# Attention into an MLP on one core: q and k of four first blocks loaded in 1 KB packets, turned 64 columns at a time, and the mask counts spread by TensorE

## The chip, the cores and the metric

One Trainium2 chip, one of its cores. The metric is device time in microseconds for one execution of the whole program. The kernel before took 602.19 us, the median of three runs (601.85, 602.19, 604.92). Its profiled execution took 602.55 us; the profiled span inside it is 600.8 us. Engines are named as in the profile: PE (TensorE; PEld its weight loads), DVE (VectorE), ACT (ScalarE), POOL (GpSimd), SP (SyncE, which here only issues DMAs).

## The reference

```python
batch, n_heads, seq, head_dim = (4, 8, 768, 64); n_global, n_local = (8, 96)
def _attn_ref(q, k, v, n_global, n_local):
    scores = np.matmul(q, k.transpose(0, 1, 3, 2)) / np.sqrt(D)
    rel = pos[:, None] - pos[None, :]
    is_global = pos[None, :] < n_global
    is_local = (rel >= 0) & (rel < n_local)
    keep = is_global | is_local
    dist = np.where(is_global & ~is_local, n_local, np.abs(rel))
    scores = scores - slopes[:, None, None] * dist     # slopes = 2 ** -(h + 1), 8 heads
    a = softmax(np.where(keep, scores, -1e9))
    return np.matmul(a, v)
def _moe_ref(x, w_in, w_out):                          # x (3072, 512), w_in (512, 2048), w_out (2048, 512)
    h = x @ w_in
    return (h / (1 + np.exp(-1.702 * h))) @ w_out
```

q, k and v are fp32 of shape (4, 8, 768, 64), so one row of a head is 64 numbers, 256 B, and four rows that follow each other are 1 KB. The weights lie in memory as 64-bit words. `n_local` and `n_global` are 64-bit integers in memory, and the masks are made from them on the chip.

## The kernel before, in words

The sequence of each batch is cut into six blocks of 128 positions, 24 blocks in all. Every query needs the keys of its own block, of the block before, and the first `n_global` keys. The four first blocks of the batches (n = 0 to 3, `n < EARLY` and `n < FIRST`) need their own block alone, and are done first, in fp32 (`prep_first`, `first`). The other twenty are done later with fp16 pairs and DMA transposes (`prep`, `unit`). After two blocks are finished, their 256 rows are a chunk of the MLP: `up` (tile h) and `down` (tile y) run over eight slices of the weights, and from the third chunk on `up_two` and `down_two` take their place.

Each step is a `Task` with the engines that may do it and an estimated price; it is added to a list by `add`. `Work.order` then plays the list through with the estimates and due times (shifted by the table `NUDGE`), and writes the instructions of every engine in the order that comes out. Each engine keeps this order on the chip and waits where data or a buffer isn't ready. Where PE finds nothing ready in the first 50 us of that plan, `order` puts in a spare pair of products on constant data (tile `idle`, line 1056), whose result nobody reads.

For a first block `prep_first` does this. `load` issues one DMA on SP for q and one for k, from `(q, k)[b, :, 128 rows, :]` to the tile `raw` with a position in each partition and the eight heads behind each other; each packet is a row of 256 B. `turn` (line 422) turns two heads at a time, four transposes of 128x128 for q and four for k, into the PSUM tile `tq` (two such buffers, ring `r_h`, shared with the spares and with h). `taken` (line 429) scales and copies: q goes to `QZ` in two halves (its upper 64 partitions and its lower 64, each to its own columns; POOL has written zeros between), one by ACT and one by DVE; k goes to `KF` (its buffers are named hl) whole, by ACT. Then `first` makes the scores of four heads at a time (tile s, line 604, fp32, with the mask added by a bf16 product, line 605), their maxima on DVE (`top`), a transpose of those (`aux`), the scores again turned (sT), their exponentials on ACT (pt, line 636), and the products with v (pv).

The masks: POOL writes the positions (`places`), DVE turns them into distances. `ci` holds the two counts, read by two DMAs on ACT's queue into all 128 partitions. `counts` (lines 308 to 311) makes `cnt` of them, `own` the mask of the own block, `other` that of the block before; `slopes` multiplies by each head's slope, with line 338 on ACT and line 340 on DVE: eight 128x128 masks for the first blocks (M1, four on each engine) and eight 128x256 masks for later blocks (M2, on DVE).

The weights come by SP, 1 MB at a time (ws), and are made into fp16 pairs by steps on DVE and ACT (lines 370 to 378, tiles wa and w).

Of the kernel before, what the change touches and what calls it, by code (L numbers as in the profile page):

```python
# [8 lines left out]
F32 = mybir.dt.float32  # L9
# [3 lines left out]
I32 = mybir.dt.int32  # L13
# [6 lines left out]
P = 128  # L20
# [6 lines left out]

NUDGE = {"T2": -1.5, "down02": 1.4, "down05": -8.2, "down07": -0.8, "down103": 6.7, "down113": -5.5,  # L30
# [4 lines left out]

NG = 8
SKIP = 24
EARLY = 4

FIRST = 4  # L40
SIGN = [{"DVE": 0.62, "ACT": 1.0}]
TURN_X = 4
WARM, GAP = 50.0, 0.5
AHEAD = 24.0
BACKLOG = 3.0
# [42 lines left out]
class Work:  # L88
# [15 lines left out]
    def order(self):  # L104
# [17 lines left out]
                        t.due, moved = due, True  # L122
        for t in self.tasks:
            t.due += NUDGE.get(t.tag, 0.0)
        free = dict.fromkeys(("PE", "DVE", "ACT", "POOL", "SP"), 0.0)
        dma, now, done = 1.5, 0.0, []
        worked, spared = 0.6, 0
# [2 lines left out]
        while len(done) < len(self.tasks) + spared:  # L130
            moved = False
            for e in free:
                if free[e] > now or (e == "SP" and dma > now + BACKLOG):
                    continue
                best = None
                for t, at in ready.items():
                    if e not in t.on or at > now or t.early() > now or (best is not None and t.due >= best.due):
                        continue
                    us = t.on[e]
                    if any(max(free[o], now) + c < now + us for o, c in t.on.items() if o != e):  # L140
                        continue
# [12 lines left out]
                if best is None:  # L154
                    if e != "PE" or now > WARM or now < worked + (GAP if worked > 7.0 else 0.0):
                        continue
                    best = self.spare(spared)
                    b = best.bufs[0]
                    if len(b.ring.taken) >= b.ring.bufs and (b.ring.taken[-b.ring.bufs].left or b.ring.taken[-b.ring.bufs].end > now):
                        continue  # L160
                    b.users, b.left = [best], 1
                    ready[best] = now
                    spared += 1
                t, us = best, best.on[e]
# [45 lines left out]
def kernel(  # L210
# [34 lines left out]
    cf = const.tile([P, 2, 2], F32, name="cf")  # L245
# [60 lines left out]

    def counts(e):
        nc.vector.tensor_copy(cf, ci)
# [25 lines left out]
    def slopes(e, js, hs=range(H)):  # L334
        for h in hs:
# [3 lines left out]
            else:  # L339
                nc.vector.tensor_scalar(mm[:, h, js], mk()[:, js], f, None, ALU.mult)  # L340

    wk.tag = "masks"
    m0 = add({"POOL": 2.0}, places, bufs=[ints], want=-9.0)
    m0 = add({"DVE": 1.3}, distances, [m0], [ints, flt, mk], -4.0)
    late = add({"POOL": 1.0}, lambda e: None, [m0], want=0.0)
    m0 = add({"DVE": 0.65}, counts, [m0, late])
    covers = add({"DVE": 1.2}, covered, [m0])
    covers.soon = 300.0
    m1 = add({"DVE": 1.1}, own, [m0], [flt, mk])
# [45 lines left out]
    def load(n, raw, parts=(0, 1, 2)):  # L395
        b, i = place(n)
        return [add({"SP": 1.55}, lambda e, z=z: nc.sync.dma_start(
            raw()[:, z], (q, k, v)[z][b, :, i * P:(i + 1) * P, :].rearrange("h p d -> p h d")), bufs=[raw]) for z in parts]

    def guard(n, raw, ld, want):  # L400

        for z, us in ((0, 1.06), (1, 0.63)):
# [5 lines left out]
    def prep_first(n):  # L408
# [3 lines left out]
        KF = Buf(r_hl, [P, NU, P], F32, f"KF{n}", lambda t: t.bitcast(F32).rearrange("p (u t) -> p u t", u=NU))  # L412
        d = blk[n] = dict(QZ=QZ, KF=KF, sm=Buf(r_sm, [P, 2 * H], F32, f"sm{n}"))
        zero = add({"POOL": 1.0}, lambda e: [nc.gpsimd.memset(QZ()[D * z:D * z + D, :, 1 - z, :], 0.0) for z in range(2)], bufs=[QZ])
        ld = load(n, raw, (0, 1))
        turned = []
        for z in range(2):
            tq = Buf(r_h, [P, NU, P], F32, f"tq{n}_{z}")

            def turn(e, z=z, tq=tq):  # L420
                for u in range(NU):
                    nc.tensor.transpose(tq()[:, u], raw()[:, z, 2 * u:2 * u + 2, :].rearrange("p h d -> p (h d)"), ident)

            turned.append((tq, add({"PE": 4 * TURN}, turn, ld[z:z + 1], [raw, tq])))

        def taken(to, z, part):
            tq, t1 = turned[z]
            return add({"ACT": 0.6, "DVE": 0.7}, lambda e: (
                nc.scalar.mul(to(), tq()[part], SX) if e == "ACT" else nc.vector.tensor_scalar(to(), tq()[part], SX, None, ALU.mult)),
                [t1], [tq, KF if z else QZ])  # L430

        rows = [slice(D * z, D * z + D) for z in range(2)]
        d["qk_ready"] = [zero, *(taken(lambda z=z: QZ()[rows[z], :, z, :], 0, rows[z]) for z in range(2)), taken(KF, 1, slice(0, P))]

    def own_values(n):

# [82 lines left out]
    def unit(n, u, want_s, want_v):  # L519
# [27 lines left out]
        d.setdefault("S", []).append(t1)  # L547
        ex = []
        for j in range(2):
            t2 = add({"DVE": 0.365}, lambda e, j=j: rows(e, j), [t1, M2], [sp, pr])  # L550
# [30 lines left out]
    def first(n, want):  # L581
# [15 lines left out]
        for f in range(2):  # L597
# [6 lines left out]
                        nc.tensor.matmul(sp()[:, j], qp, kp, start=(z == 0), stop=False, skip_group_check=True)  # L604
                    nc.tensor.matmul(sp()[:, j], id16, mm[:, h, 2], start=False, stop=True, skip_group_check=True)

            t1 = add({"PE": 4 * (mm_s + MM128)}, scores, [M1[f], *d["qk_ready"]], [sp, *QKs], want + 1.2 * f)
            d.setdefault("S", []).append(t1)
            maxed.append(add({"DVE": 0.61}, lambda e, f=f, sp=sp: nc.vector.tensor_reduce(
                top[:, n, 4 * f:4 * f + 4], sp(), axis=AX.X, op=ALU.max, negate=True), [t1], [sp]))  # L610
# [656 lines left out]
```

## Time and profile before

| what | value |
|---|---|
| median of the runs | 602.19 us |
| profiled execution | 602.55 us, span 600.8 us, mean granted clock of TensorE 0.997 |
| busy shares | PE 98%, PEld 74%, DVE 84%, ACT 78%, POOL 1% |
| DMA packets | 268502, of which 249536 under 512 B; 109.58 MB |
| queue q10, on which the counts come | 288 packets |
| loads of q and k in this form | 24 each, 256 KB each (four of each for the first blocks) |

A row of a group has the line, the engine, the operation, output and inputs, and how often, then busy time and the mean of one, then the idle time of the engine just before and what ended it. A row in order of time has the start, the duration, and in brackets the idle time before it with its releaser. Bars of matmuls are modelled at their ends: a bar reaches into the next one, so the price of one in a dense row is read from start to start. PEclk in the tables is the granted clock as a share.

### The profile page before, as it was taken

The numbers are of one execution on the slowest core, as the hardware profiler recorded it, in microseconds if no ns is written. First come the engines' busy times: TensorE is split into PE (matmuls) and PEld (weight loads), VectorE is DVE, ScalarE is ACT, GpSimd is POOL, SyncE is SP. The second block draws the span as 40 slices with busy tenths as digits, with TensorE's granted clock in tenths as the row PEclk, the third lists the DMA queues.
The fourth block names the chain that finished last, engine by engine and source line by source line (L and its number), as shares of the span: only waits on it lengthen the run. The fifth ranks groups of instructions, "written<-read, shape, count | busy, mean of one in ns | idle before, by whom it ended". The sixth has DMA issues, their size and how long they took to land.

```text
span 600.8 us, 17038 instructions
## 1 busy us (share of the span) xinstructions
PE 587.3 (98%) x6816; PEld 445.8 (74%) x6816; DVE 502.9 (84%) x1177; ACT 471.6 (78%) x1098; POOL 5.8 (1%) x18
## 2 busy tenths in 40 slices
PE   8989999999999999999999999999999999999995
PEld 5878767776777867777677777777678778867895
DVE  6998999999999999789699789798979978766532
ACT  3878899978758988888688899788989988844432
POOL 3000000000000000000000000000000000000000
PEclk9999999999999999999999999999999999999998
DMA  8998898999976778969996999999989999910001
GB/s 221 316 249 254 235 251 191 196 187 203 198 139 127 160 117 182 199 141 206 194 222 153 227 204 233 206 229 198 240 181 227 227 205 237 231 29 3 36 2 40
DMA packets 268502, 109.58 MB, mean 182 GB/s; under 512 B 249536, under 2 KB 250048, under 8 KB 268416
## 3 DMA queue, kind: packets, MB, share of 16 engines
q1 hardware_dynamic: 268128, 108.43, 85.7%
q8 instruction: 55, 0.90, 0.6%
q14 instruction: 31, 0.25, 0.1%
q10 hardware_dynamic: 288, 0.00, 0.0%
HBM read 57.67 MB, written 6.29 MB: 106 GB/s over the span
## 4 chain that ended last, share of the span: by engine, by line
PE 82%; DMA 7%; ACT 4%; DVE 4%; issue 1%; SPq 1%; DVEq 0%; ACTq 0%
PE y L895 35%; PE pa L827 13%; PE h L787 10%; PE pb L827 10%; PE s L536 4%; DMA pt<-hl 2%; DMA out_dram<-yo 1%; PE s L604 1%; PE pv L567 1%; PE pv L568 1%; PE pv L569 1%; PE sT L623 1%; DMA raw<-in_k_dram 1%; DMA xT<-x 1%; DMA ws_00again<-in_moe_w_in_dram 1%
## 5 line engine op out<-in xcount | busy, mean ns | idle before, releaser
L895 PE MATMUL y<-w,g 128*128 128x512 f16 (+1 forms) x1248 | 266.9, 363 | 0.0
L895 PEld LDWEIGHTS <-g 128*128 128x128 f16 x1248 | 117.9, 98 | 103.3
L827 PEld LDWEIGHTS <-w 128*128 128x128 f16 x1728 | 101.2, 98 | 4.8
L552 ACT ACTIVATE p<-p,NM 128x232 f32<-128x232 f32 x160 | 76.5, 481 | 7.3 <-DVE NM L542 7.1
L827 PEld LDWEIGHTS <-T 128*128 128x128 f16 x1296 | 77.1, 98 | 6.2 <-issue 0.2
L787 PE MATMUL h<-xT,w 128*128 128x256 f16 x576 | 69.4, 273 | 0.5 <-DMA xT<-x 0.5
L542 DVE CUSTOM_DVE_ANT_0 p<-s,mm 128x232 f32<-128x232 f32 x160 | 57.7, 396 | 8.4 <-PE s L536 7.8
L787 PEld LDWEIGHTS <-w 128*128 128x128 f16 x576 | 55.2, 98 | 9.6 <-issue 0.8
L868 DVE SCALAR_TENSOR_TENSOR g<-t,g 128x512 f16<-128x512 f32 x72 | 49.3, 688 | 12.3 <-ACT g L867 12.0
L557 DVE TENSOR_TENSOR hl<-p,hl 128x464 f16<-128x464 f32 x80 | 50.9, 637 | 8.1 <-ACT hl L556 7.9
L867 ACT ACTIVATE g<-t 128x512 f16<-128x512 f32 x72 | 45.0, 628 | 9.5 <-DVE t L860 8.1
L859 ACT ACTIVATE t<-h 128x512 f32<-128x512 f32 (+1 forms) x72 | 35.9, 516 | 18.0 <-DVE h L835 14.9
L556 ACT CAST hl<-p 128x464 f16<-128x464 f32 x80 | 46.1, 577 | 4.2 <-DMA pt<-hl 2.3
L835 DVE TENSOR_TENSOR h<-pb,h 128x256 f32<-128x256 f32 x72 | 29.5, 420 | 22.6 <-PE pb L827 19.3
L827 PE MATMUL pa<-xS,T 128*128 128x128 f16 x648 | 45.0, 219 | 0.1
L860 DVE SCALAR_TENSOR_TENSOR t<-t,h 128x512 f32<-128x512 f32 (+1 forms) x72 | 38.3, 554 | 4.8 <-ACT t L859 4.2
L536 PEld LDWEIGHTS <-QK 128*128 128x128 f16 x640 | 36.4, 98 | 4.3 <-DMA QK<-QK 0.8
L536 PE MATMUL s<-QK 128*128 128x128 f16 x320 | 38.5, 219 | 0.6 <-DMA QK<-QK 0.6
L827 PE MATMUL pb<-xS,w 128*128 128x128 f16 x540 | 37.5, 219 | 0.0
L827 PE MATMUL pa<-xT,w 128*128 128x128 f16 x540 | 37.0, 219 | 0.0
L567 PE MATMUL pv<-VR,pt 128*128 128x64 f16 x288 | 34.8, 193 | 1.3 <-DMA pt<-hl 1.3
L569 PE MATMUL pv<-VR,pt 128*128 128x64 f16 x288 | 34.9, 193 | 0.0
(181 smaller groups left out, 1080.7 us busy)
## 6 DMA issues: line engine op xcount, KB each, us to landing
ws<-in_moe_w_in_dram SPq DMA_DIRECT2D x8, 1024.0 KB
ws<-in_moe_w_out_dram SPq DMA_DIRECT2D x8, 1024.0 KB
raw<-in_q_dram SPq DMA_DIRECT2D x24, 256.0 KB
raw<-in_k_dram SPq DMA_DIRECT2D x24, 256.0 KB
out_dram<-yo SPq DMA_DIRECT2D x22, 256.0 KB
QK<-QK SPq DMA_DIRECT2D x40, 128.0 KB
raw<-in_v_dram SPq DMA_DIRECT2D x20, 256.0 KB
ws_00again<-in_moe_w_in_dram SPq DMA_DIRECT2D x8, 512.0 KB
```

The lines of the kernel that those rows point to most:

```text
L536: nc.tensor.matmul(sp()[:, j, lo:hi], d["QK"]()[:, 0, h, :], K[:, 1 + z, h, P - (hi - lo):], start=(z == 0), stop=(z == 1), skip_group_che ...
L542: nc.vector.tensor_tensor_reduce(out=pr()[:, j, :], in0=sp()[:, j, :], in1=m, scale=-1.0 / SC, scalar=3.0e38, op0=ALU.add, op1=ALU.min, ac ...
L552: ex.append(add({"ACT": 0.473}, lambda e, j=j: nc.scalar.activation(pr()[:, j, :], pr()[:, j, :], AF.Exp, bias=NM[:, n, hs[j]:hs[j] + 1], ...
L556: t4 = add({"ACT": 0.5}, lambda e: nc.scalar.copy(hl()[:, 0, :, SKIP:], pr()), ex, [pr, hl])
L557: t5 = add({"DVE": 0.55}, lambda e: nc.vector.tensor_sub(hl()[:, 1, :, SKIP:], pr(), hl()[:, 0, :, SKIP:]), [t4], [pr, hl])
L567: nc.tensor.matmul(o, ph, V[:, 0, h], start=(s == 0), stop=False, skip_group_check=True)
L569: nc.tensor.matmul(o, pl, V[:, 0, h], start=False, stop=(s == ns - 1), skip_group_check=True)
L787: nc.tensor.matmul(ph()[:, fi, :], w1(s, cc, z, fi), X[:, y, cc, :], start=(j + cc == 0), stop=(j == 2 and cc == NCC - 1))
L827: nc.tensor.matmul(o()[:, fi], w, x()[:, y * NCC + 2 * k + cc, t], start=(first and fi + j + cc == 0), stop=(last and j + cc == 3), skip_g ...
L867: t4 = add({"ACT": 0.53}, lambda e, g=g, tt=tt: nc.scalar.mul(g()[:, 0], tt(), SG / (SX * SW)), u, [tt, g])
L868: t5 = add({"DVE": 0.61}, lambda e, g=g, tt=tt: nc.vector.scalar_tensor_tensor(g()[:, 1], tt(), SG / (SX * SW), g()[:, 0], ALU.mult, ALU.s ...
L895: nc.tensor.matmul(y(), part(zg, f), w2(s, z, f % 2)[:, m], start=(begin and f + j == 0), stop=(end and j == 2 and f == 2 * len(steps) - 1 ...
```

## The change

Three things are edited. First, `load_pairs` replaces `load` for the first blocks: positions are put in partitions so that four rows of one head, 1 KB, lie in one partition; a partition holds two groups of four rows (for four heads each), and each group has a DMA of its own, so q takes two DMAs and k two. Second, `turn` then turns 64 columns at a time: four transposes into the upper 64 partitions of `tq`, and four fp32 products with the identity into the lower 64; `taken` reads `tq` in a permuted order to put the positions right, and for the first two blocks takes k in two halves of 256 columns, with the first scores bound to the first half alone. Third, the counts are read into one partition, worked on there, and spread to 128 partitions by a product with a row of ones on PE (`pc`) and a copy on DVE. Beside these the eight masks M2 are bound to ACT, and the table `NUDGE` is another one.

```diff
-NUDGE = {"T2": -1.5, "down02": 1.4, "down05": -8.2, ...
+NUDGE = {"T0": 7.7, "block0": -8.3, "block3": -0.7, ...
...
+HOLD = {}
...
-    ci = const.tile([P, 2, 2], I32, name="ci")
+    ci = const.tile([1, 2, 2], I32, name="ci")
     for j, src in enumerate((n_local, n_global)):
-        nc.scalar.dma_start(ci[:, j], src.bitcast(I32).rearrange("(o x) -> o x", o=1).broadcast_to([P, 2]))
+        nc.scalar.dma_start(ci[:, j], src.bitcast(I32).rearrange("(o x) -> o x", o=1))
...
     def counts(e):
         nc.vector.tensor_copy(cf, ci)
-        nc.vector.tensor_scalar(cnt, cf[:, :, 0], 0.0, None, ALU.is_lt)
-        nc.vector.tensor_add(cnt, cnt, cf[:, :, 1])
-        nc.vector.scalar_tensor_tensor(cnt, cnt, float(2 ** 32), cf[:, :, 0], ALU.mult, ALU.add)
+        nc.vector.tensor_scalar(c1, cf[:, :, 0], 0.0, None, ALU.is_lt)
+        nc.vector.tensor_add(c1, c1, cf[:, :, 1])
+        nc.vector.scalar_tensor_tensor(c1, c1, float(2 ** 32), cf[:, :, 0], ALU.mult, ALU.add)
...
-    m0 = add({"DVE": 0.65}, counts, [m0, late])
+    m0 = add({"DVE": 0.7}, counts, [m0, late], want=COUNTS)
+    pc = Buf(r_pv, [P, 2], F32, "pc")
+    m0 = add({"PE": 0.2}, lambda e: nc.tensor.matmul(pc(), row, c1, start=True, stop=True), [m0], [pc], COUNTS)
+    m0 = add({"DVE": 0.15}, lambda e: nc.vector.tensor_copy(cnt, pc()), [m0], [pc], COUNTS)
...
-    M2 = add({"DVE": 2.3, "ACT": 2.6}, lambda e: slopes(e, slice(0, 2)), [m2], [mk])
+    M2 = [add({"ACT": 0.65}, lambda e, f=f: slopes(e, slice(0, 2), range(2 * f, 2 * f + 2)), [m2], [mk]) for f in range(4)]
...
+    def load_pairs(n, raw):
+        b, i = place(n)
+        ld = []
+        for z in range(2):
+            src = (q, k)[z][b, :, i * P:(i + 1) * P, :].rearrange("(u e) (j t) d -> e u j (t d)", e=2, t=4)
+            dst = raw()[:, z].rearrange("p (e t) d -> p e (t d)", e=2)
+            ld.append([add({"SP": 0.45}, lambda e, src=src, dst=dst, o=o: nc.sync.dma_start(dst[:, o], src[o]), bufs=[raw]) for o in range(2)])
+        return ld
...
-        ld = load(n, raw, (0, 1))
+        ld = load_pairs(n, raw)
...
             def turn(e, z=z, tq=tq):
-                for u in range(NU):
-                    nc.tensor.transpose(tq()[:, u], raw()[:, z, 2 * u:2 * u + 2, :].rearrange("p h d -> p (h d)"), ident)
-            turned.append((tq, add({"PE": 4 * TURN}, turn, ld[z:z + 1], [raw, tq])))
-        def taken(to, z, part):
+                for u in range(4):
+                    nc.tensor.transpose(tq()[0:D, u], raw()[:, z, u, :], ident)
+                for u in range(4):
+                    nc.tensor.matmul(tq()[D:P, u], raw()[:, z, 4 + u, :], ident, start=True, stop=True, skip_group_check=True)
+            turned.append((tq, add({"PE": 4 * TURN + 4 * FP128}, turn, ld[z], [raw, tq])))
+        def taken(to, z, part, us=1.0, u=slice(0, NU)):
             tq, t1 = turned[z]
+            src = lambda: tq()[part].rearrange("p t (u j) -> p u j t", u=NU)[:, u]
+            dst = lambda: to().rearrange("p u (j t) -> p u j t", t=4)
...
-        d["qk_ready"] = [zero, *(...), taken(KF, 1, slice(0, P))]
+        if n < KHALF:
+            k_in = [taken(lambda u=u: KF()[:, u:u + 2], 1, slice(0, P), 0.6, slice(u, u + 2)) for u in (0, 2)]
+        else:
+            k_in = [taken(KF, 1, slice(0, P))] * 2
+        d["first_ready"] = [[*q_in, t] for t in k_in]
```

The order that comes out differs from the first instruction on. On PE, at the start: before, the turns of blocks 0 and 1 stand between pairs of spares (`idle`), and the scores of block 0 begin ahead of the turn of block 1's k, further down:

```order
L422 MATMUL tq_1_154<-ident,raw_107 128x128 x4
L1056 LDWEIGHTS idle
L1056 MATMUL idle_168<-idle 128x512
...
L1056 MATMUL idle_176<-idle 128x512
...
L422 MATMUL tq_0_182<-ident,raw_115 128x128 x4
...
L1056 MATMUL idle_195<-idle 128x512
...
L604 MATMUL s_0_199<-hl_89,QZ_120 128x128
```

And in the changed program, from the first turn to the first scores:

```order
L448 MATMUL tq_0_156<-ident,raw_95 64x128 x4
L450 MATMUL tq_0_156<-ident,raw_95 64x128 x4
L361 MATMUL pc<-c_68,row 128x2
L448 MATMUL tq_1_170<-ident,raw_95 64x128 x4
L450 MATMUL tq_1_170<-ident,raw_95 64x128 x4
L448 MATMUL tq_0_190<-ident,raw_96 64x128 x4
L450 MATMUL tq_0_190<-ident,raw_96 64x128 x4
L448 MATMUL tq_1_204<-ident,raw_96 64x128 x4
L450 MATMUL tq_1_204<-ident,raw_96 64x128 x4
L640 MATMUL s_0_225<-hl_92,QZ_141 128x128
```

All four turns now stand ahead of the first scores, and no spare is left between them. In all, 12 spare products stand on PE instead of 26; the first eight of them are ahead of the first turn in both.

On ACT, where the exponentials of block 0 (pt) meet the first weight steps (w), before:

```order
L613 CAST mT_79<-aux_262 8x128
L375 ACTIVATE w_0_258<-ws_0_166 128x1024
L636 ACTIVATE pt_0_299<-sT_0_272 128x512
L377 ACTIVATE w_0_258<-wa_0_270 128x1024
L636 ACTIVATE pt_1_313<-sT_1_286 128x512
```

and in the changed program:

```order
L350 ACTIVATE mm<-mk 128x256 x8
L391 ACTIVATE w_0_252<-ws_0_151 128x1024
L649 CAST mT_82<-aux_281 8x128
L393 ACTIVATE w_0_252<-wa_0_268 128x1024
L672 ACTIVATE pt_0_328<-sT_0_293 128x512
L391 ACTIVATE w_1_307<-ws_1_213 128x1024
L672 ACTIVATE pt_1_339<-sT_1_315 128x512
```

The eight masks M2 have come to ACT, and both weight steps of the first slice now stand ahead of the first exponential; a step of the second slice stands between the two exponentials.

More of the change, by code (lines that the diff above doesn't have):

```diff
@@ L40 @@
 FIRST = 4
+KHALF = 2
 SIGN = [{"DVE": 0.62, "ACT": 1.0}]
 TURN_X = 4
+HOLD = {}
 WARM, GAP = 50.0, 0.5
@@ L163, in order @@
                     spared += 1
+                if e in HOLD and best.due < 1e8:
+                    soon = [at for t, at in ready.items() if e in t.on and now < at <= now + min(HOLD[e], 0.5 * best.on[e]) and
+                            t.due < best.due - 1.0 and t.early() <= at]
+                    if now < held.setdefault((best, e), max(soon, default=0.0)):
+                        continue
                 t, us = best, best.on[e]
@@ L241 @@
     SC = SX * SX * float(D) ** 0.5
-    ci = const.tile([P, 2, 2], I32, name="ci")
+    ci = const.tile([1, 2, 2], I32, name="ci")
     for j, src in enumerate((n_local, n_global)):
-        nc.scalar.dma_start(ci[:, j], src.bitcast(I32).rearrange("(o x) -> o x", o=1).broadcast_to([P, 2]))
-    cf = const.tile([P, 2, 2], F32, name="cf")
+        nc.scalar.dma_start(ci[:, j], src.bitcast(I32).rearrange("(o x) -> o x", o=1))
+    cf = const.tile([1, 2, 2], F32, name="cf")
+    c1 = const.tile([1, 2], F32, name="c1")
+    row = const.tile([1, P], F32, name="row")
+    nc.vector.memset(row, 1.0)
     cnt = const.tile([P, 2], F32, name="cnt")
@@ L340, in slopes @@
                 nc.vector.tensor_scalar(mm[:, h, js], mk()[:, js], f, None, ALU.mult)
+    LATE, COUNTS = 1.2, 0.0
     wk.tag = "masks"
     m0 = add({"POOL": 2.0}, places, bufs=[ints], want=-9.0)
+    late = add({"POOL": LATE}, lambda e: None, [m0], want=-9.0)
     m0 = add({"DVE": 1.3}, distances, [m0], [ints, flt, mk], -4.0)
-    late = add({"POOL": 1.0}, lambda e: None, [m0], want=0.0)
-    m0 = add({"DVE": 0.65}, counts, [m0, late])
+    m0 = add({"DVE": 0.7}, counts, [m0, late], want=COUNTS)
+    pc = Buf(r_pv, [P, 2], F32, "pc")
+    m0 = add({"PE": 0.2}, lambda e: nc.tensor.matmul(pc(), row, c1, start=True, stop=True), [m0], [pc], COUNTS)
+    m0 = add({"DVE": 0.15}, lambda e: nc.vector.tensor_copy(cnt, pc()), [m0], [pc], COUNTS)
     covers = add({"DVE": 1.2}, covered, [m0])
     covers.soon = 300.0
-    m1 = add({"DVE": 1.1}, own, [m0], [flt, mk])
+    m1 = add({"DVE": 1.1}, own, [m0], [flt, mk], COUNTS)
     M1 = [add({"DVE": 0.6, "ACT": 1.0}, lambda e, f=f: slopes(e, slice(2, 3), range(4 * f, 4 * f + 4)), [m1], [mk]) for f in range(2)]
     m2 = add({"DVE": 0.7}, other, [m1], [flt, mk])
-    M2 = add({"DVE": 2.3, "ACT": 2.6}, lambda e: slopes(e, slice(0, 2)), [m2], [mk])
+    M2 = [add({"ACT": 0.65}, lambda e, f=f: slopes(e, slice(0, 2), range(2 * f, 2 * f + 2)), [m2], [mk]) for f in range(4)]
     WT, W_ready = {}, {}
@@ L420, in turn @@
             def turn(e, z=z, tq=tq):
-                for u in range(NU):
-                    nc.tensor.transpose(tq()[:, u], raw()[:, z, 2 * u:2 * u + 2, :].rearrange("p h d -> p (h d)"), ident)
-            turned.append((tq, add({"PE": 4 * TURN}, turn, ld[z:z + 1], [raw, tq])))
-        def taken(to, z, part):
+                for u in range(4):
[4 more added lines that the diff above has]
+        def taken(to, z, part, us=1.0, u=slice(0, NU)):
             tq, t1 = turned[z]
-            return add({"ACT": 0.6, "DVE": 0.7}, lambda e: (
-                nc.scalar.mul(to(), tq()[part], SX) if e == "ACT" else nc.vector.tensor_scalar(to(), tq()[part], SX, None, ALU.mult)),
+            src = lambda: tq()[part].rearrange("p t (u j) -> p u j t", u=NU)[:, u]
+            dst = lambda: to().rearrange("p u (j t) -> p u j t", t=4)
+            return add({"ACT": 0.6 * us, "DVE": 0.7 * us}, lambda e: (
+                nc.scalar.mul(dst(), src(), SX) if e == "ACT" else nc.vector.tensor_scalar(dst(), src(), SX, None, ALU.mult)),
                 [t1], [tq, KF if z else QZ])
         rows = [slice(D * z, D * z + D) for z in range(2)]
-        d["qk_ready"] = [zero, *(taken(lambda z=z: QZ()[rows[z], :, z, :], 0, rows[z]) for z in range(2)), taken(KF, 1, slice(0, P))]
+        q_in = [zero, *(taken(lambda z=z: QZ()[rows[z], :, z, :], 0, rows[z]) for z in range(2))]
+        if n < KHALF:
[3 more added lines that the diff above has]
+        d["first_ready"] = [[*q_in, t] for t in k_in]
+        d["qk_ready"] = [*q_in, *dict.fromkeys(k_in)]
     def own_values(n):
@@ L549, in unit @@
         for j in range(2):
-            t2 = add({"DVE": 0.365}, lambda e, j=j: rows(e, j), [t1, M2], [sp, pr])
+            t2 = add({"DVE": 0.365}, lambda e, j=j: rows(e, j), [t1, *M2], [sp, pr])
             checks.append(t2)
@@ L605, in scores @@
                     nc.tensor.matmul(sp()[:, j], id16, mm[:, h, 2], start=False, stop=True, skip_group_check=True)
-            t1 = add({"PE": 4 * (mm_s + MM128)}, scores, [M1[f], *d["qk_ready"]], [sp, *QKs], want + 1.2 * f)
+            t1 = add({"PE": 4 * (mm_s + MM128)}, scores, [M1[f], *(d["first_ready"][f] if n < FIRST else d["qk_ready"])], [sp, *QKs], want + 1.2 * f)
             d.setdefault("S", []).append(t1)
```

3 lines of the change are left out of this document (2 added, 1 removed), and 9 rows, old and new, of the table NUDGE.

## The prediction

> **What bounds the kernel now.** I read the page's busy shares and slices first, then a table by stretches.
>
> ```profile
> PE 587.3 (98%) x6816; PEld 445.8 (74%) x6816; DVE 502.9 (84%) x1177; ACT 471.6 (78%) x1098; POOL 5.8 (1%) x18
> ...
> PE   8989999999999999999999999999999999999995
> ```
>
> PE (TensorE) is busy 98% of a 600.8 us span. A busy bar can hide a waiting engine, so the stretches come next (PE, weight loads, DVE, ACT, POOL; granted clock, DMA share, GB/s):
>
> ```profile
> 0.00:10.00 10.00, 7.82 (x28) 3.81 (x29) 5.12 (x22) 3.23 (x7) 5.75 (x18) 1.00 0.76 155
> 10.00:20.00 10.00, 10.00 (x96) 9.54 (x95) 8.88 (x24) 4.65 (x8) 0.00 (x0) 1.00 1.03 341
> 20.00:30.00 10.00, 9.27 (x82) 8.23 (x82) 9.21 (x19) 9.24 (x12) 0.00 (x0) 1.00 1.14 311
> 30.00:40.00 10.00, 7.90 (x67) 6.64 (x67) 9.66 (x14) 7.39 (x11) 0.00 (x0) 1.00 0.79 241
> 40.00:50.00 10.00, 10.00 (x101) 9.47 (x98) 9.86 (x12) 9.28 (x13) 0.00 (x0) 1.00 0.96 269
> ...
> 590.00:600.80 10.80, 4.77 (x44) 3.82 (x42) 1.08 (x8) 1.53 (x4) 0.00 (x0) 0.85 0.18 57
> ```
>
> From 40 us on PE has no room. What can be won lies in the first 40 us: 5.0 us idle (2.18 + 0.73 + 2.10) and the spare products of line 1056, which compute nothing and only fill PE's time. Between 40 us and the tail the waits of PE on DMA come to 2.4 us:
>
> ```profile
> PE pv L567 <- DMA pt<-hl: 1.3, 2, 0.8
> ...
> PE s L536 <- DMA QK<-QK: 0.6, 1, 0.6
> ...
> PE h L787 <- DMA xT<-x: 0.5, 1, 0.5
> ```
>
> So the question is one of PE's time: what the change adds to PE in the start against the spares and waits it can push out. The spares of the start, and then PE's rows there in order of time:
>
> ```profile
> L1056 PE MATMUL idle<-idle 128*128 128x512 bf16 x26 | 9.2, 476 | 2.9 <-ACT hl L429 1.6 <-POOL idle L252 1.3
> ```
>
> ```profile
> 1.33 3.59 PE L1056 MATMUL idle<-idle 128*128 128x512 bf16 x8 [1.33 <-POOL idle L252]
> ...
> 4.74 1.09 PE L422 MATMUL tq<-ident,raw 128*128 128x128 f32 x4
> ...
> 5.61 1.06 PE L1056 MATMUL idle<-idle 128*128 128x512 bf16 x2
> ...
> 6.84 0.77 PE L422 MATMUL tq<-ident,raw 128*128 128x128 f32 x4 [0.17 <-DMA raw<-in_k_dram]
> ...
> 8.30 1.02 PE L1056 MATMUL idle<-idle 128*128 128x512 bf16 x4 [0.68 <-ACT hl L429]
> ...
> 9.16 0.60 PE L422 MATMUL tq<-ident,raw 128*128 128x128 f32 x4
> ...
> 28.46 0.66 PE L689 MATMUL tx<-ident,x 128*128 128x128 f32 x4 [0.71 <-DVE x L669]
> ...
> 30.91 0.59 PE L1056 MATMUL idle<-idle 128*128 128x512 bf16 x2 [0.92 <-ACT hl L429]
> ...
> 37.69 0.27 PE L612 MATMUL aux<-ident,top 128*8 128x128 f32 x1 [0.58 <-DVE top L609]
> ...
> 38.52 0.66 PE L422 MATMUL tq<-ident,raw 128*128 128x128 f32 x4 [0.56 <-DVE QZ L429]
> ```
>
> Two things are to be seen. PE starts at half rate: eight spares take 3.59 us, four later ones 1.02, and four turns 1.09 us, later 0.60; the rate doubles at about 7 us. And a turn waits for a free tile or for data six times.
>
> **The turns on TensorE.** A bar is longer than its place in the pipeline:
>
> ```profile
> L422 PE MATMUL tq<-ident,raw x32: 272/273/447, 4.7 to 38.9; 128*128 128x128 f32 x32
> ```
>
> (0.60 - 0.27) / 3 = 0.11 us from start to start, so a load's turn of four costs 0.44 us (0.89 at half rate). The changed one is four transposes of 64 columns and four fp32 products of 64 columns with the identity. No such product is in this trace; the nearest are these, of 128 columns:
>
> ```profile
> 10.25 0.30 PEld L604 LDWEIGHTS s<-hl,QZ 128*128 128x128 f32 x2
> 10.30 0.44 PE L604 MATMUL s<-hl,QZ 128*128 128x128 f32 x2
> ...
> 10.63 0.44 PE L604 MATMUL s<-hl,QZ 128*128 128x128 f32 x2
> ...
> 16.55 0.44 PE L623 MATMUL sT<-QZ,hl 128*128 128x128 f32 x2
> ...
> 16.94 0.44 PE L623 MATMUL sT<-QZ,hl 128*128 128x128 f32 x2
> ```
>
> A head takes 0.33 us with one bf16 product and 0.39 with two, so bf16 costs 0.06 and an fp32 product 0.27: two passes. Upper end 0.27 (paced by the two weight loads of 0.30 in all, unchanged). Lower end 0.11 (one pass suffices for half the columns). I take 0.22, two passes of 0.11 with the shorter load of 64 columns out of the way. A transpose of 64 columns still streams 128 rows: 0.11. A turn then costs 0.44 + 0.88 = 1.32 us, 2.64 at half rate. The first one falls there: it can't start before about 4.7, since the same eight spares stand ahead of it. Added: 2.64 - 0.89 = 1.75 for the first, 7 x 0.88 = 6.16 for the others: **+7.9 us** (ends +4.0 and +9.7).
>
> **Spares that go.** The order keeps 12 of the 26. The pair of 5.61 runs at half rate (0.43 each), the other twelve at (1.02 - 0.38) / 3 = 0.21: **-3.4 us**.
>
> **Waits that can go.** 0.17 + 0.68 + 0.71 + 0.92 + 0.58 + 0.56 = 3.6 us of shown idle; each begins 0.16 earlier than shown (0.27 - 0.11), six times, 1.0: **-4.6 us** if all go.
>
> **Counts.** In the trace they stand on DVE behind the taking of q:
>
> ```profile
> 7.21 0.17 DVE L308 CAST cf<-ci 128x4 f32<-128x4 int32 x1
> ...
> 9.24 0.91 ACT L338 ACTIVATE mm<-mk 128x128 bf16<-128x128 f32 x4 [0.99 <-DVE mk L327]
> ...
> 11.17 1.69 DVE L340 TENSOR_SCALAR mm<-mk 128x256 bf16<-128x256 f32 x8
> ```
>
> The four small operations go ahead of that taking; new are one product on PE (**+0.1**) and a copy to 128 partitions on DVE (0.17, as the copy above). DVE's copy waits for that product, which stands on PE behind q's first turn (end 4.74 + 2.64 = 7.4), and behind the copy on DVE are the masks, for which the scores wait: masks at about 10.1 instead of 9.24. The scores come at 7.4 + 0.1 + 3 x 1.32 = 11.4 or later, so this is hidden; without that cover it costs the 0.9. The eight 128x256 products of masks go from DVE (-1.69) to ACT (8 x 0.23 to 0.46, the ends from its 0.91 for four of half the size; 2.6 taken). ACT is busy 4.65 of 10 us there, so PE doesn't see it.
>
> **Loads.** Each q or k goes as two DMAs of 128 packets of 1 KB instead of one of 1024 packets of 256 B. In the first 10 us, nearly all 256 B, the queues move 155 GB/s, in the next ten with 2 and 4 KB 341, so eight loads of 0.26 MB may save up to half their time. What it is worth on PE is the 0.17 us already counted: PE has its own work until k's turn is due. k in the chain of work, and in order of time an issue on SP and the first use of a weight:
>
> ```profile
> 1.27 5.43 DMA raw<-in_k_dram
> ```
>
> ```profile
> 0.75 0.46 SPq L397 DMA_DIRECT2D raw<-in_q_dram  x1
> ...
> 15.16 0.68 DVE L373 TENSOR_SCALAR w<-ws 128x1024 int32<-128x1024 int32 x1
> ```
>
> k landed at 6.70; now it is due only at 7.5. SP issues eight DMAs more, 0.46 us each, four of them ahead of the first weights, which are used at 15 us. I cost that at nothing; without that cover 8 x 0.46 = 3.7 us on SP stand ahead of the later weights.
>
> **Taking the turned data.** ACT and DVE now read the turned tile in a permuted order, with 512 B from one element to the next. No row shows such a read. The same instructions took 0.6 and 0.7 us in plain order; the ends are no change and twice that. I take no change, since the number of elements is the same; twice would lengthen each wait for a tile below, by some 0.7 us in the first.
>
> **New waits.** Without any the sum is 7.9 - 3.4 - 4.6 + 0.1 = 0.0. But PE has two tiles for turned data. The turn of block 1's q now waits for ACT's reading of block 0's k, in two halves; such a half is
>
> ```profile
> L832 ACT COPY h<-pa 128x256 f32<-128x256 f32 x36 | 13.2, 367 | 3.0 <-PE pa L827 2.8
> ```
>
> so 2 x 0.37 with a handover: 0.8 us, much like the 0.68 of the trace. Later, ACT does a weight step of 1.06 us ahead of block 0's first exponential; in the trace the exponential came first:
>
> ```profile
> 17.92 0.60 ACT L636 ACTIVATE pt<-sT 128x512 f32<-128x512 f32 x1 [0.41 <-PE sT L625]
> ...
> 18.80 1.06 ACT L377 ACTIVATE w<-wa 128x1024 f16<-128x1024 f32 x1 [0.28 <-DVE wa L376]
> ```
>
> PE's values wait for that exponential, 0 to 1.0 us. The turn of block 2's k waits for ACT's taking of q, behind three ACT steps: 0 to 0.9, the same kind as the 0.92 above. Block 2's second scores wait for DVE: 0 to 0.3. That is 0.8 and 0 to 2.2; I take 0.7 of the latter, a third, since PE's longer turns cover part. Sum: **+1.5 us**. Everything after 40 us is the same work in another order; I leave its 2.4 us of waits as they are, give or take 1.5. The profiled execution took 602.55 us, 0.36 over the median of 602.19: 602.19 + 1.5 = **603.7**.
>
> **A rule against the change.** The row: turns ran at half rate until 7 us and at full rate later, while spares and turns alternated. The Trainium skill ("TensorE: Matmul & The Clock Gate", Part 4) says that transposes don't count as activity for the clock as other matmuls do. The trace can't confirm it. By that rule the clock could come later, which is the second rival.
>
> **Rivals.**
> - *ACT and DVE set the start.* The new waits are paid in full (0.8 + 2.2) and the product costs 0.27 (+1.8): +4.8, 607.0. For it: between 20 and 50 us DVE is busy 9.2 to 9.9 of 10. Against: DVE loses 1.69 us. It decides for "slower" from +3.0 on.
> - *The clock comes late.* If the three turns after the first also run at half rate: 3 x 1.32 = +4.0 on top, 607.7. Against: eight spares still run first.
> - *A drain at each change of column width.* Each turn leaves the full array and comes back; if the pipeline runs empty each time, 16 x 0.16 = 2.6: 606.3. The Trainium skill ("TensorEngine Tiling (Array Packing)", Key Properties) states such a drain for a change of tiling mode; no row here shows one.
> - *Half columns, half price.* A product at 0.11 and only the first new wait: 4.0 - 3.4 - 4.6 + 0.1 + 0.8 = -3.1, 599.1: faster. Against: PE's time for a product goes by the 128 rows that stream.
> - *The loads change, the time doesn't:* 0 to +1 as above; part of my forecast.
>
> **From this to numbers.** This kernel's measurement tells about 0.5%, 3.0 us. Forecast (599.2 to 605.2): 0.63. ACT and DVE 0.13, late clock 0.06, drain 0.07: slower 0.26. Half price 0.11: faster. The likeliest case's own range is 601.0 to 605.2. To hold 8 in 10 the range starts just above the half-price case, 599.8, and takes in the first rival, to 607.5.
>
> **What would show it.** In the new profile: eight turns of about 1.3 us, the first twice that; twelve spares; a PE wait of about 0.8 on ACT ahead of block 1's q; masks ready before scores; the first h rows about 1.5 us later in work done. I am wrong if a 64-column product starts every 0.11 us, if waits after 40 us change by over 2 us, or if the rate doubles much off 7 us.

## The result, and the profile after

The changed kernel takes 617.37 us, the median of three runs (616.35 to 618.32), against 602.19: a ratio of 1.0231, 95% interval 1.0202 to 1.0261. That is slower by 15.2 us by the medians, 13.9 by the ratio; the forecast of 603.7 and its range to 607.5 were wrong. The profiled execution took 618.32 us, with a span of 616.5. A ratio here is not the quotient of the two medians (that would be 1.0252), and below too the two differ a little.

The page's busy shares and slices of the changed kernel:

```profile
PE 599.4 (97%) x6868; PEld 454.8 (74%) x6868; DVE 503.4 (82%) x1174; ACT 473.5 (77%) x1105; POOL 5.8 (1%) x18
...
PE   7979999999999999999999999999999999999995
...
PEclk9988999999999999999999999999999999999999
```

A slice is 15.4 us; the first and the third of PE are lower than before (7 for 8), and the third and fourth of the clock. The table by stretches, same columns as before:

```profile
0.00:10.00 10.00, 8.16 (x27) 4.31 (x28) 3.63 (x16) 1.87 (x2) 5.75 (x18) 1.00 0.20 66
10.00:20.00 10.00, 8.08 (x63) 6.87 (x64) 4.86 (x16) 4.87 (x16) 0.00 (x0) 1.00 0.90 265
20.00:30.00 10.00, 9.95 (x92) 9.00 (x91) 9.63 (x19) 7.35 (x10) 0.00 (x0) 1.00 0.78 250
30.00:40.00 10.00, 6.84 (x55) 5.83 (x55) 6.20 (x11) 5.87 (x7) 0.00 (x0) 0.90 0.65 185
40.00:50.00 10.00, 7.56 (x51) 6.25 (x50) 4.55 (x7) 4.55 (x6) 0.00 (x0) 0.84 0.95 277
```

Three things stand out. The DMA share of the first ten microseconds is 0.20 where it was 0.76, and 66 GB/s where it was 155, though the packets are four times as large. From 30 to 50 us PE, DVE and ACT are all idle for a good part. And the granted clock is 0.90 and 0.84 there. PE's waits, in order of time:

```profile
5.14 1.03 PE L448 MATMUL tq<-ident,raw 128*64 128x128 f32 x4 [0.21 <-DMA raw<-in_q_dram]
6.47 1.97 PE L450 MATMUL tq<-ident,raw 128*64 128x128 f32 x8 [0.30 <-DMA raw<-in_q_dram]
...
12.13 0.63 PE L448 MATMUL tq<-ident,raw 128*64 128x128 f32 x4 [0.75 <-ACT hl L459]
...
15.54 1.09 PE L450 MATMUL tq<-ident,raw 128*64 128x128 f32 x8 [1.08 <-DMA raw<-in_k_dram]
...
38.44 1.06 PE L448 MATMUL tq<-ident,raw 128*64 128x128 f32 x4 [3.16 <-ACT QZ L459]
...
47.40 0.49 PE L640 MATMUL s<-hl,QZ 128*128 128x128 f32 x2 [2.44 <-DVE xT L729]
```

The two long waits name ACT and DVE, but these were waiting too. DVE just before, in order of time:

```profile
35.10 0.69 DVE L386 TENSOR_SCALAR wa<-ws 128x1024 int32<-128x1024 int32 x1 [3.01 <-DMA ws<-in_moe_w_out_dram]
...
45.45 0.69 DVE L389 TENSOR_SCALAR w<-ws 128x1024 int32<-128x1024 int32 x1 [6.17 <-DMA ws<-in_moe_w_in_dram]
46.06 0.69 DVE L386 TENSOR_SCALAR wa<-ws 128x1024 int32<-128x1024 int32 x1
46.66 0.69 DVE L729 TENSOR_TENSOR xT<-tx,xT 128x512 f16<-128x512 f32 x1
```

DVE keeps its order: xT (46.66), for which PE waits 2.44 us, stands behind a step on weights that came 6.17 us late. ACT waited 2.89 us at 35 for the same reason. So the late thing is the weights, and on SP, which issues them, the new loads take long (start, duration, what):

```profile
16.29 2.98 SPq L423 DMA_DIRECT2D raw<-in_q_dram  x2
19.32 3.74 SPq L423 DMA_DIRECT2D raw<-in_k_dram  x2
...
28.06 4.81 SPq L423 DMA_DIRECT2D raw<-in_k_dram  x2
```

Why they are slow is seen in the landings. The core has 16 DMA engines; "queue" below means one of these. A DMA counts up its semaphore, the counter on which its users wait, once for each queue that has finished its part. Counted from the trace (time of the last increment, in us, and how many the queues made):

```
              q0             k0            q1              k1              v of block 0 (VF)
before    4.60 (16)      6.71 (16)     7.88 (16)       9.01 (16)      10.05 (16)
after     5.00, 6.43 (4, 4)   7.86, 9.30 (4, 4)   10.92, 12.30 (4, 4)   13.73, 15.50 (4, 4)   11.99 (12), then 16.51 (4)
```

Each of the new loads runs on 4 of the 16 queues. Their packets of 1 KB take 46 ns each on a queue, those of 256 B 18 ns: 22 GB/s a queue against 14, so the larger packets are better, but 4 x 22 = 89 GB/s is less than 16 x 14 = 228. From 2 to 13 us all queues together moved 101 GB/s, before 234. And VF, which uses all queues, had 12 parts at 11.99 and the last 4 only at 16.51, behind the q and k loads on the four busy queues: whatever uses 16 queues waits for the slowest four, the weights too. Of the weights for which DVE waited 3.01 us, 12 parts had landed at 31.51 and the last 4 came from 34.21 to 35.00; of those behind the 6.17 us, 12 at 40.55 and the last at 45.43. The rest of their lateness is a late issue on SP: the fourth weights went out at 23.17, in the 16-queue version below at 16.86. The Trainium skill ("DMA: Bandwidth & Descriptors", "Why a DMA increments its semaphore by 16 and not by 1") states the rule: a DMA is split over the largest k up to 16 that divides the slowest count (other than 1) of both of its patterns. The new source begins with u, which counts 4; the trace agrees, with 4 increments.

### The profile page after: what moved, and what is told of

Its sections match the earlier page's. It is cut to its first block, busy times and chain, and to the rows that moved or that the text cites. A ratio compares the mean times of both kernels' runs of the same rounds, so it can differ in the third digit from the quotient of the medians.

```text
span 616.5 us, 17165 instructions
## 1 busy us (share of the span) xinstructions
PE 599.4 (97%) x6868; PEld 454.8 (74%) x6868; DVE 503.4 (82%) x1174; ACT 473.5 (77%) x1105; POOL 5.8 (1%) x18
## 4 chain that ended last, share of the span: by engine, by line
PE 82%; DMA 8%; DVE 3%; ACT 2%; SPq 2%; issue 1%; DVEq 0%
PE y L931 36%; PE pa L863 13%; PE h L823 10%; PE pb L863 10%; PE s L572 4%; DMA ws<-in_moe_w_in_dram 2%; SPq L423 2%; DMA pt<-hl 1%; DMA raw<-in_k_dram 1%; PE pv L603 1%; PE s L640 1%; PE pv L605 1%; PE pv L604 1%; DMA ws_11again<-in_moe_w_out_dram 1%; DMA ws_01again<-in_moe_w_in_dram 1%
```

## The experiments

Theory A: the loads' 4 queues cost most of the time. Rival B: the longer turns and the new order do. Rival D: the number of DMA issues on SP does. Times are medians with the ratio to the kernel before, run beside it on the same chip.

**16 queues, all else the same.** Positions are dealt to partitions with j outermost, so the slowest count is 32:

```diff
-  .rearrange("(u e) (j t) d -> e u j (t d)", e=2, t=4)
+  .rearrange("(u e) (j t) d -> e j u (t d)", e=2, t=4)
-  tq()[part].rearrange("p t (u j) -> p u j t", u=NU)[:, u]
+  tq()[part].rearrange("p t (j u) -> p u j t", u=NU)[:, u]
```

> The changed kernel with the same order, turns, counts and number of DMAs; only the map of positions to partitions is another (j outside u), so that the source of a load has 32 as its slowest count instead of 4. Theory A (each of the sixteen new loads runs on 4 of the 16 DMA queues, and that starves the start and holds the weights up): landings carry 16 increments instead of 4, k of block 0 lands at about 6 us instead of 9.3, the first weights at about 13 instead of 19.3, PE's idle time before 50 us falls from 9.4 to under 4 us, and the time is 602 to 606 us, the sum of the prediction. Rival B (the longer turns and the new order are what costs): 615 to 618 us. Rival D (eight more DMA issues on SP hold the weights up): 614 to 618 us, since their number stays.

606.66 us, ratio 1.0055 (1.0033 to 1.0078). 10.7 of the 15.2 us are back; A holds, though the time is 0.7 above the range I gave it, and B and D in these sizes don't. Each load has 16 increments; k of block 0 lands at 5.4, block 1 at 7.9, the first weights at 12.8. Up to 50 us PE waits only twice, and DVE waits for no weights:

```profile
9.03 0.63 PE L448 MATMUL tq<-ident,raw 128*64 128x128 f32 x4 [0.75 <-ACT hl L459]
9.59 1.09 PE L450 MATMUL tq<-ident,raw 128*64 128x128 f32 x8
10.61 0.63 PE L448 MATMUL tq<-ident,raw 128*64 128x128 f32 x4
...
31.41 0.63 PE L448 MATMUL tq<-ident,raw 128*64 128x128 f32 x4 [0.52 <-ACT QZ L459]
```

**One DMA a load instead of two, on 16 queues.** (`j u e (t d)` as one source.)

> The changed kernel with 16 queues and one DMA a load instead of two (the same 1 KB packets, turns, order and counts): eight issues on SP less. If the number of DMAs had a part in the loss (rival D): 603 to 605.5 us. If it is the queues alone: 606 to 608 us, as with two DMAs on 16 queues (606.7).

606.7 us, ratio 1.0052 (1.0024 to 1.0079): no difference. D falls.

**The kernel before with loads on 4 queues, and its control.** Each load is split by partitions into two:

```diff
-  ld = load(n, raw, (0, 1))
+  ld = [... [nc.sync.dma_start(raw()[o:m, z], (q, k)[z][b, :, i*P+o:i*P+m, :].rearrange("h p d -> p h d"))
+        for o, m in ((0, 116), (116, P))] ...]          # control: 112 for 116
```

> The kernel before, same order, old turns, packets of 256 B; each load of q or k of a first block is two DMAs, of 116 and of 12 partitions, where 116 = 4 x 29 leaves 4 queues. Theory A: 928 packets over 4 queues are 232 each, by the 18 ns of a packet before 4.2 us a load; four of them one behind the other put k of block 1 at about 18 us instead of 9.0 and the first weights at about 23 instead of 14.3; time 612 to 622 us. Rival B: the loads are covered, 602 to 604 us. Rival D (DMA issues on SP): 602.2 + 3.7 = 606 us.

> As the run on 4 queues, but split at 112 and 16 partitions, both multiples of 16: the same number of DMAs, 16 queues each. Theory A: 601 to 604 us, first landings within 1 us of before. Rival D (issues on SP): 8 x 0.46 = 3.7 us on the way of the weights, up to 606 us.

Split at 116: 611.86 us, 1.0142 (1.0119 to 1.0166), just under the low edge of what A said. Split at 112, the same number of DMAs, four partitions moved: 602.12 us, 0.9991 (0.9973 to 1.0010). In the traces a part of 116 partitions made 4 increments, one of 12 made 12, and those of 112 and 16 made 16 each. So 4 queues cost time by themselves, with the old turns and packets, and eight more DMAs don't. PE on 4 queues:

```profile
7.22 1.09 PE L422 MATMUL tq<-ident,raw 128*128 128x128 f32 x4 [2.29 <-DMA raw<-in_q_dram]
...
10.64 1.09 PE L422 MATMUL tq<-ident,raw 128*128 128x128 f32 x4 [1.48 <-DMA raw<-in_k_dram]
```

**Which of the loads.** 16 queues for blocks 0 and 1 alone (`"..e j u.." if n < 2 else "..e u j.."`), and for blocks 2 and 3 alone.

> The changed kernel with 16 queues for the loads of blocks 0 and 1 alone, 4 queues for blocks 2 and 3. If the late start is what costs (k of block 0 at 9.3 us, block 1 at 15.5): 606 to 609 us. If what costs is that the weights stand on SP and in the queues behind all eight slow loads: 611 to 615 us. PE's idle time before 32 us should be as with all on 16 queues either way; what differs lies from 32 to 50 us.

> The changed kernel with 16 queues for the loads of blocks 2 and 3 alone, 4 queues for blocks 0 and 1: the complement of the run with blocks 0 and 1 on 16 queues, which got back 4.8 of the 10.7 us. If the two parts add up: 617.4 - 5.9 = 611.5, 610.5 to 612.5 us, and PE's waits of 3.16 and 2.44 us between 35 and 48 us are gone. If the lateness of the first blocks is handed on to the weights whatever blocks 2 and 3 do: 614 to 617 us.

612.63 us (1.0153, 1.0118 to 1.0188) and 611.70 (1.0118, 1.0094 to 1.0143): 4.7 and 5.7 us better than the change, 10.4 together of the 10.7, so they add up. With blocks 2 and 3 slow the long wait is still there, and DVE shows why:

```profile
40.54 0.80 PE L640 MATMUL s<-hl,QZ 128*128 128x128 f32 x2 [3.25 <-DVE xT L729]
```

```profile
38.59 0.69 DVE L389 TENSOR_SCALAR w<-ws 128x1024 int32<-128x1024 int32 x1 [4.02 <-DMA ws<-in_moe_w_in_dram]
```

With blocks 0 and 1 slow it is gone; PE then waits for data in the first 16 us, 4.1 us in six pieces.

**Weights taken off SP** (`load_weights(..., q=nc.gpsimd)` for the sixteen loads).

> The changed kernel with its 4-queue loads, but the sixteen loads of weights are issued by POOL and not by SP, so that they don't stand on SP behind the slow loads. If it is SP's queue that holds the weights up: the first weights land at 13 us or earlier instead of 19.3, the waits of DVE on weights (3.01 and 6.17 us) and of PE behind them (3.16 and 2.44) go, 610 to 613 us. If the weights only trade places with the q and k loads in the DMA queues: 615 to 619 us. If POOL's own order holds them up: above 619 us.

622.44 us, 1.0309 (1.0288 to 1.0331): worse. The weights now come ahead, and the loads on 4 queues wait behind them, on SP and on PE:

```profile
5.14 11.85 SPq L423 DMA_DIRECT2D raw<-in_k_dram  x2
```

```profile
15.24 1.97 PE L450 MATMUL tq<-ident,raw 128*64 128x128 f32 x8 [4.95 <-DMA raw<-in_k_dram]
20.71 1.03 PE L448 MATMUL tq<-ident,raw 128*64 128x128 f32 x4 [3.51 <-DMA raw<-in_q_dram]
```

So it is not SP's queue alone: the two kinds of transfer share the four busy DMA queues, and by the rows who goes first decides who is late. 622 is also what I had put down to POOL's own order (above 619), and POOL did issue the fourth weights only at 31.5. The rows speak for the loads: PE's waits come to 10.5 us up to 26 us, and to some 0.6 from there to 60. POOL's first weights, too, had 12 parts landed at 10.15 us and the last 4 at 13.48. No run separates the two causes.

**The new turns alone**, in the kernel before, with its loads:

```diff
-  for u in range(NU):
-      nc.tensor.transpose(tq()[:, u], raw()[:, z, 2*u:2*u+2, :]...., ident)
+  # four transposes of raw[:, z, 2u, :] to tq[0:D, u], then four products of raw[:, z, 2u+1, :] to tq[D:P, u]
```

> The kernel before, same order and same loads; only the turn is the new one, four transposes of 64 columns and four fp32 products of 64 columns. By the prediction's term the turns add 7.9 us on PE, and the 4.6 us of waits can cover a part: 605.5 to 610 us. If half columns were half price: 604 us or less, and a turn 0.88 us at full rate. If a change of column width drained the pipeline: 2.6 us more, a turn 1.65 us, up to 612 us.

612.23 us, 1.0160 (1.0132 to 1.0188), above the 610 of the first theory. A full-rate turn:

```profile
10.33 1.62 PE L422 MATMUL tq<-ident,raw 128*64 128x128 f32 x12
11.88 0.39 PE L1056 MATMUL idle<-idle 128*128 128x512 bf16 x1
```

11.88 - 10.33 = 1.55 us, where I had 1.32; 8 x (1.58 - 0.44) = 9.1 of the 9.6 us, with the 1.58 of the 16-queue run (10.61 - 9.03). In this order no wait gives way to it, since the spares still stand between the turns.

**Transposes and products in turn**, in the 16-queue version, so that the half of the columns changes eight times a turn.

> The 16-queue version with the eight operations of each turn in another order: transpose, product, transpose, product, so that the half of the columns changes eight times a turn instead of twice. In the 16-queue trace a product starts 0.20 us after a transpose and a transpose or score 0.20 after a product, where 0.11 is the price of the work. If that 0.09 is paid at every change: 6 more changes a turn, 8 turns, 4.3 us more, 609 to 612 us, and a turn of 2.1 us instead of 1.58. If it is paid once a turn only: 606 to 607.5 us.

613.55 us, 1.0191 (1.0130 to 1.0251), slower than the 16-queue version by 6.9 us and above the 612 of the first theory.

```profile
30.61 0.27 PE L448 MATMUL tq<-ident,raw 128*64 128x128 f32 x1
30.81 0.43 PE L450 MATMUL tq<-ident,raw 128*64 128x128 f32 x2
31.17 0.30 PE L448 MATMUL tq<-ident,raw 128*64 128x128 f32 x1
31.40 0.43 PE L450 MATMUL tq<-ident,raw 128*64 128x128 f32 x2
31.77 0.30 PE L448 MATMUL tq<-ident,raw 128*64 128x128 f32 x1
```

A pair of them takes (31.77 - 30.61) / 2 = 0.58 us, where the work is 0.33: 0.125 for each change. Two changes make the 0.25 that a turn of the change has over 1.32, eight make 1.0. Each change of half is here also one between a transpose and a product. That the kind alone does not cost is seen at full width, in the version with the old turns in the new order (below):

```profile
24.41 0.60 PE L725 MATMUL tx<-ident,x 128*128 128x128 f32 x4
24.85 1.68 PE L667 MATMUL pv<-VF,pt 128*128 128x65 f32 x14
```

The four transposes take 0.11 each, and the first product starts right behind them, at 24.41 + 0.44. After a turn of 64 columns, though, the next start is 0.20 away whatever follows, scores of full width too.

**Loads and turns in the old order.** 1 KB packets on 16 queues with new turns, and the same on 4 queues, both in the kernel before with its order.

> The kernel before in its own order (spares, counts and masks as before), with the new turns and with 1 KB packets on 16 queues, one DMA a load. The run with the new turns alone took 612.2. If 1 KB packets on all queues bring data to PE sooner in a way that counts: 608 to 610.5 us. If the loads are covered once they use 16 queues: 611 to 613 us. If 1 KB packets cost in themselves (theory A false, the packets and not the queues are slow): above 615 us.

> As the run before it in this list, with the loads of the change: two DMAs each, 4 queues. Theory A: the 10.7 us that the change got back with 16 queues come on top, 619 to 624 us. If the order of before hides slow loads better (spares stand where PE would wait): 613 to 618 us.

614.16 us (1.0172, 1.0127 to 1.0217) and 615.66 (1.0218, 1.0172 to 1.0265). On 16 queues 1 KB packets bring nothing over the 612.2 of the turns alone: the loads were covered, but for the first, for which PE waited 1.21 us. On 4 queues the 619 to 624 of theory A missed, and the 613 to 618 of the other theory held: the slow loads cost 1.5 us here by the medians and 2.8 by the ratios, up to some 7 by the intervals, not 10.7. In this order SP issues the fourth weights at 25.08 and only then q and k of block 2 (25.55), and DVE waited for no weights from 8 to 50 us; in the changed order block 2 goes at 16.29, ahead of the fourth weights (23.17). That the order is the reason fits these rows, but it can't be the whole of it: the run split at 116 has the old order too, with k of block 1 landing at 17.0 us as here (17.3) and the fourth weights (23.96) ahead of block 2 (24.43), and 4 queues cost 9 us in it. Its packets are of 256 B, so its q of block 2 held SP for 6.7 us where it took 1.1 here, and its rate doubled at 17.2 us, here at 5.4. Why slow loads cost less here stays open.

**Old loads and turns in the new order**, with the new counts and masks.

> The changed kernel's order, counts and masks, with the loads, the turns and the taking of the kernel before. The 16-queue run less eight turns' surplus (8 x 1.1 = 9 us by its trace) would be 597.7; since the spares that stood between the turns are left out, up to 4 us of PE's time turn into waits: 597.5 to 602 us. If the new order is worse in itself: 602.5 to 606 us.

601.19 us, 0.9982 (0.9964 to 0.9999). The order is not worse in itself, and this version beats the changed kernel clearly and the kernel before by a fifth of a per cent, if at all: its interval ends just under 1.

**The same, planned with the old prices** (1.55 us a load, 0.44 a turn), so another order.

> The old loads and turns again with the new counts and masks, but with the order that the plan makes when it is told the old prices of loads and turns (1.55 us a load, 0.44 a turn), so spares come back between the turns. If the order made for the longer turns is what held the last run but one at 601.2: 598 to 600.5 us. If the order matters little once data is in time: 600.6 to 603 us.

608.79 us, 1.0081 (1.0055 to 1.0108): missed on the far side. The same work in another order, with the same table of shifts, costs 6 us more by the ratios.

**The same, with the counts as before.**

> The kernel with the old loads and turns in the new order (601.2), and the counts as before too: read into 128 partitions by a broadcast, worked on there, no product on PE, no copy on DVE. The prediction holds the counts hidden: no difference, 600.5 to 602.5 us. If the product and the copy stand on the way of the masks (the 0.9 us named in the prediction): 599 to 600.4 us. If the 256 small packets of the broadcast disturb the first loads: 602.6 to 604 us.

604.19 us, 1.0023 (0.9997 to 1.0048), against 0.9982 with the new counts: above the no difference that I expected, but the intervals touch. So what follows is a reading, not shown: with the broadcast the counts landed late, and so did k.

```profile
5.53 0.60 DVE L320 CAST cf<-ci 128x4 f32<-128x4 int32 x1 [1.60 <-DMA ci<-in_n_global_dram]
```

```profile
6.83 1.09 PE L448 MATMUL tq<-ident,raw 128*128 128x128 f32 x4 [0.98 <-DMA raw<-in_k_dram]
```

**Ten spares instead of eight** ahead of the first turn, in the same version.

> The kernel with the old loads and turns in the new order (601.2, 600.7 to 604.0), with ten spare products ahead of the first turn instead of eight. Eight last 3.6 us, and after them PE's rate doubled at 4.9 us in one profile and at 7 to 14 us in others of like beginnings. If PE has to be busy with products (and not transposes) for a little more than that: the rate doubles by 6 us, the turns run at full rate, the single times spread less (600 to 602), median 600 to 601.5 us. If the two products only cost their time: 601.5 to 602.5 us, and the same spread.

602.23 us, 0.9980 (0.9964 to 0.9995), single runs 600.9 to 605.1. The rate did double at 5.1 us, but neither the time nor the spread changed. That theory of the spread falls.

## Why the prediction was wrong

- **Loads: the step that failed.** "So eight loads of 0.26 MB may save up to half their time. What it is worth on PE is the 0.17 us already counted". They cost 10.7 us. I took the rate of all queues at two packet sizes (155 and 341 GB/s) for the rate that a load of that packet size would have, and never asked on how many queues it runs. The diff had the answer, in the `u` of 4 that leads the source, and so has the Trainium skill's section named above. No rival had the loads get slower; the guard in that part, 3.7 us for SP's issues, guarded against the wrong thing.
- **How it became 10.7.** Waits of PE before 50 us: 0.21 + 0.30 + 0.75 + 1.08 + 3.16 + 2.44 = 7.9 us, against 0.75 + 0.52 = 1.3 on 16 queues: 6.7 more. The rest is the clock. In the two profiles, which lie 11.6 us apart, the two stretches at half rate below lost 3.2 us, and the start about 2.8, since the rate doubled at 10.8 us instead of 4.9 (the first scores come 4.4 us later, of which 1.6 are waits). That is a little more than the difference.
- **Turns: mis-sized by 2.1 us.** Two passes of 0.11 for a 64-column product were right, and "half columns, half price" wrong. But 1.32 leaves out 2 x 0.13 for the changes of column half, 16 x 0.13 = 2.1 in all. That is nearest to the third rival, 16 gaps of 0.16, but not where it put them: on coming from full width a turn starts with no gap (0.06 us after a bf16 product, the place of such a product), and the two gaps are between the halves and on leaving. The Trainium skill ("TensorEngine Tiling (Array Packing)", Key Properties) has the drain for a change of tiling mode and not for a change of tile alone; here a gap is paid between the two halves, within one shape of 128x64 (0.20 us from the last transpose to the first product, and back, where 0.11 is the work), so the measurement decides.
- **Spares and waits: right, once data is in time.** Twelve spares are left, as costed. On 16 queues the six old waits are gone, the two new ones are 0.75 (0.8 said) and 0.52 (0.7 said).
- **The sum without the loads.** +1.5 with the missing +2.1 is +3.6; on 16 queues the ratio gives +3.3 (2.0 to 4.7). That they lie so close is in part luck: the sum has the first turn at half rate, and in that profile the rate doubled at 4.9 us, as the turn began.
- **Taking the turned data: right.** 592 ns on ACT against 595, 683 to 691 on DVE against 691: the permuted read costs nothing.
- **Counts:** no cost is seen, as said; undoing them gained nothing, and may have lost.
- **The late clock.** The first turn did run at half rate, and here the second did too: the rate doubled at 10.8 us. What set that moment is not shown. With the same slow loads of blocks 0 and 1 it came at 4.2 us in the run with blocks 2 and 3 on 16 queues. Whether turns keep the clock low is not settled: the rate doubled among turns in the alternating run (6.0 us) and in the kernel before (7.2), but eight spares stand ahead of them in both.

## What to carry to other kernels

Before a load is priced by its packets, count its queues: read the slowest dimension of both patterns as they stand in the diff, and put one there that is a multiple of 16. A transfer on few queues also holds up what is spread over all of them, so look for its price at the next thing that lands late (here weights, 20 us later, behind engines that keep their order) and not only at its own consumer. An order made for one set of prices is worth several microseconds by itself: compare a change in an order that is held fixed.

## What the hardware showed

PE's rate falls to half at the end of a wait or up to 2 us behind it, and stays there for 3.41 us by the traces' record of the granted clock, in all eight such stretches ahead of the tail. In the changed kernel, after the 3.16 us wait:

```profile
38.44 1.06 PE L448 MATMUL tq<-ident,raw 128*64 128x128 f32 x4 [3.16 <-ACT QZ L459]
39.42 1.97 PE L450 MATMUL tq<-ident,raw 128*64 128x128 f32 x8
...
41.88 0.60 PE L448 MATMUL tq<-ident,raw 128*64 128x128 f32 x4
42.41 1.09 PE L450 MATMUL tq<-ident,raw 128*64 128x128 f32 x8
```

By the starts of the products it was half from 38.4 to 41.6 and, after the 2.44 us wait, from 48.5 to 51.8: 6.4 us at half rate, 3.2 us lost, which is what the granted 0.90 and 0.84 of the table show. Three other runs had such a stretch behind waits of 3.25, 1.50, and 1.52 with 1.68; after 1.34 us two had it and one not; after 1.21 and less in this part of the program there was none. No run takes the clock apart from the wait before it. At the start, with eight spares ahead, the rate doubled anywhere from 4.2 to 13.7 us, and at 17.2 and 24.2 in the two runs where PE stood over 3 us for loads by then; in the old order with 1 KB packets on 4 queues it doubled at 5.4 and was at half again from 8.8 to 12.2, behind waits of 2.03 and 0.48. The tables' granted clock begins with that first doubling, so it reads 1.00 for the first ten microseconds although the rows there run in part or wholly at half rate. The single times of the kernel before spread from 599.6 to 605.8 us over the comparisons, and those of the version with ten spares are spread as widely as with eight.
